# Silu in one activation for two token blocks, and weight chunks 29 to 40 assembled in SBUF instead of PSUM

## The chip, the cores and the metric

The kernel runs on one core of one Trainium2 chip. The core has five engines with an in-order queue each: TensorE (PE, matmuls, with its weight loads shown as PEld), VectorE (DVE), ScalarE (ACT), GpSimd (POOL) and SyncE (SP, which here only starts transfers). The metric is the time of one execution on the device in microseconds; lower is better.

## The reference

Three parts follow one another. All arithmetic of the reference is at float32 or better, and the weights come as float64.

```python
# attention: 2 x 8 heads, 768 tokens, head size 64; a query sees the keys of its hash bucket
scores = where(bucket(q) == bucket(k), q @ k.T / 8, -1e9)
x = softmax(scores) @ v                      # -> 1536 tokens x 512
# first feed-forward block, d_ff = 1536
xn = x / sqrt(mean(x * x) + 1e-6) * rms_g
g, val = xn @ w_gate, xn @ w_val
x = (g * (1 / (1 + exp(-g))) * val) @ w_out
# second feed-forward block, d_ff = 2048
r = maximum(x @ w_in, 0)
out = (r * r) @ w2_out
```

## The kernel before

**Precision.** Every float32 operand of a feed-forward matmul is split in a high part, which is rounded to the matmul's input format, and a low part, the rest. A product is then three matmuls: high x high, high x low, low x high. So weights and activations need two tiles each, and DVE makes the low parts by a subtraction (line 314).

**Token blocks.** The 1536 tokens are four blocks of 384 (`TB`). The first feed-forward block runs over blocks 0 and 1 while the second half of attention still runs (run 0), then over blocks 2 and 3 (run 1). The second feed-forward block then takes all four. Within a run the loop goes over 12 slices `f` of 128 hidden units. For a slice and a block PE makes the gate (`in_pe`, 12 matmuls of 384 columns, line 1012), then the value, also line 1012. Every two slices the output product follows (line 1108), whose result DVE adds to an accumulator in SBUF (line 1133).

**A gate and a value.** `gate_t` (line 1023) takes tanh(g/2) on ScalarE out of the PSUM bank into a tile `mt`. `gate_u` (line 1027) multiplies (mt + 1) with g, still in its bank, on DVE, into a tile `mu`. `val_u` (line 1032) multiplies with 0.5 and with the value. `y_hi` (a cast, ScalarE or GpSimd) and `y_lo` (a subtraction on DVE) split the result for the output product. There are three `mt` buffers and four `mu` buffers.

**Weights.** The weights are loaded as raw float64 chunks of 128 x 512 (512 KB each) and put together as float32 by integer operations: an absolute value of the upper words on ScalarE (`w_abs`, line 956), then four steps on DVE (`w_f32`: a clamp, line 962, a shift, line 967, and two that merge bits of the raw words, lines 972 and 976), a rounding cast (`w_hi`) and a subtraction (`w_lo`, line 314, DVE). There are 104 chunks, in the order of use: 36 of run 0 (gate, value, output for each slice), 36 of run 1 and 32 of the second block. There are three raw buffers (`wraw`). The tile on which the steps work is one of four in SBUF (`wv`), or, for chunks with an index in `WP = (6, 40)`, a PSUM bank (`mo`): `apart(m)` says which, and then the cast can only be ScalarE's, since GpSimd doesn't reach PSUM in this kernel. The banks `mo` are taken in turn, eight of them from the end of attention on, and the matmuls' results need them too.

**Order.** Nothing is ordered by the compiler. Each operation is given to a planner (`Plan`) with a rank, the engines that may do it, a cost on each (`D`, `A`, `P`, `T`), the buffers that it takes and frees, and whether it uses an SBUF port that DVE and GpSimd share (`port`). The planner plays a list schedule through by these costs and emits the instructions in that order; each engine then runs its own in order and waits by semaphores. A changed cost changes the order of everything that comes later.

Of the kernel before, what the change touches and what calls it, by code (L numbers as in the profile page):

```python
# [10 lines left out]
F32 = mybir.dt.float32  # L11
# [5 lines left out]
AF = mybir.ActivationFunctionType  # L17
ALU = mybir.AluOpType
# [3 lines left out]
B, H, S, D = 2, 8, 768, 64  # L22
# [7 lines left out]
TB = 384  # L30
# [24 lines left out]
WR = 3  # L55
WV = 4

WP = (6, 40)
MB = (3, 4)
G = 2  # L60

# [181 lines left out]
def tile_hash_attention_moe(  # L243
# [19 lines left out]
    nc = tc.nc  # L263
# [14 lines left out]
    where = {}  # L278
# [18 lines left out]
    add = plan.op  # L297
# [638 lines left out]
    def apart(m):  # L936

        return m in mats[WP[0]:WP[1]]

# [77 lines left out]
    def in_pe(eng, st, m, blk):  # L1017
        st["p"] = mo()[:, 0:TB]
        gemm_in(st["p"], m, xT[m[0], blk])

    def gate_t(eng, st):
        st["t"] = where["work"].tile([128, TB], F32, tag="mt", name="mt", bufs=MB[0])
        nc.scalar.activation(st["t"], st["p"], AF.Tanh, scale=0.5)

    def gate_u(eng, st, us):
        us["u"] = where["work"].tile([128, TB], F32, tag="mu", name="mu", bufs=MB[1])
        nc.vector.scalar_tensor_tensor(
            out=us["u"], in0=st["t"], scalar=1.0, in1=st["p"], op0=ALU.add, op1=ALU.mult
        )

    def val_u(eng, st, us):
        nc.vector.scalar_tensor_tensor(  # L1032
            out=us["u"], in0=us["u"], scalar=0.5, in1=st["p"], op0=ALU.mult, op1=ALU.mult
        )

    def relu(eng, st):
        st["t"] = where["work"].tile([128, TB], F32, tag="mt", name="mt", bufs=MB[0])
        nc.scalar.activation(st["t"], st["p"], AF.Relu)  # L1038

    def square(eng, st, us):  # L1040
        us["u"] = where["work"].tile([128, TB], F32, tag="mu", name="mu", bufs=MB[1])
        nc.vector.tensor_tensor(out=us["u"], in0=st["t"], in1=st["t"], op=ALU.mult)  # L1042
# [17 lines left out]
    us_of = {}  # L1060

    def plan_y(key, rank, ub, us, st=None, tb=None):
        p, ring, _ = y_place(key)
        yb = ("y",) + key
        add(
            lambda e: y_hi(e, key, us, st), rank, r=[p, ("u", key)], use=[ub] + ([tb] if tb else []),
            new=[(ring, yb)], w=[("yh", key)], A=0.413, P=(0.481, 0.3),
        )
        add(
            lambda e: y_lo(e, key, us), rank, r=[("yh", key)], use=[ub, yb], w=[("yl", key)],  # L1070
            D=(0.47, H_LO), port=True,
        )

    def plan_in(what, m, blk, n, rank):
        st, b = {}, ("in", m, blk)
        which, f = m[0], m[1]
        add(
            lambda e: in_pe(e, st, m, blk), rank, new=[("mo", b)], T=2.08,
            use=[("w", m), ("xT", which, blk)], r=[("wl", m)] + [("xT", which, blk, c) for c in range(4)],
        )  # L1080
        rank += R_AFT
        if what == "val":
            us, ub = us_of.pop(blk), ("mu", blk, f)
            add(lambda e: val_u(e, st, us), rank, use=[b, ub], w=[("u", (1, blk, f))], D=0.47)
            plan_y((1, blk, f), rank, ub, us)
            return
        tb = ("mt", m, blk)
        us = {}
        if what == "gate":
            us_of[blk] = us  # L1090
            add(lambda e: gate_t(e, st), rank, r=["work"], use=[b], new=[("mt", tb)], A=0.385)
            add(
                lambda e: gate_u(e, st, us), rank, use=[b, tb], new=[("mu", ("mu", blk, f))], D=0.47,
            )
        else:
            ub = ("mu 2", blk, f)
            add(lambda e: relu(e, st), rank, r=["work"], use=[b], new=[("mt", tb)], A=0.385)
            add(lambda e: square(e, st, us), rank, use=[tb], new=[("mu", ub)], D=0.47, port=True)
            plan_y((2, blk, f), rank, ub, us, st, tb)
# [127 lines left out]
    def plan_all():  # L1227
# [30 lines left out]
        for x in products():  # L1258
            rank = J0 + spent / RATIO
            if x[0] == "out":  # L1260
                _, which, run, blk, fs, d = x
                ms = [(which, f, 2 if which == 1 else 1, run) for f in fs]
            else:
                ms = [x[1]]
            for m in ms:
                if m not in done:
                    done.add(m)
                    plan_weights(m, rank + R_W)
            if x[0] == "out":
                plan_out(which, run, blk, fs, d, rank)  # L1270
                spent += (0.49 if which == 1 else 0.65) * len(fs)
            else:
                plan_in(x[0], x[1], x[2], x[3], rank)
                spent += 1.96
# [60 lines left out]
```

## Time and profile before

| | |
|---|---|
| median of 3 runs | 837.7 us (836.83 to 839.05) |
| the profiled execution | 836.23 us |
| its span, first to last instruction | 834.4 us |
| mean granted clock of TensorE over the span | 0.982 of full speed |
| busy: PE, DVE, ACT, POOL | 793.3, 705.2, 452.4, 223.8 us |

The busy times are sums over the whole span. Attention fills about the first 325 us, with the first feed-forward block's run 0 woven into it; run 1 and the second block follow. A row of the timeline gives the start, the duration, the engine, the line, the operation with output and input tiles, and in brackets how long the engine stood idle before it and what ended that. An instruction's duration overlaps a little with the next one's on the same engine, so the step from start to start says what one costs in a full queue.

### The profile page before, as it was taken

Reading aid. Unit: us, or ns where it says so; the run is one execution under the profiler, and the core shown is the slowest. Engines: PE = TensorE matmul, PEld = TensorE weight load, DVE = VectorE, ACT = ScalarE, POOL = GpSimd, SP = SyncE. Lnnn points to the kernel's source line nnn. Section 1 sums busy time; section 2 is a strip of 40 time slices with the busy share of each in tenths; the row PEclk is TensorE's granted clock in tenths of the full one; section 3 lists DMA queues with packets and bytes.
Section 4 is the critical chain, followed back from the end, with each engine's and each line's share of the span. In section 5 each row is a group of like instructions: output and inputs, shape, how many; then the busy total and the mean of one; then the engine's idle time right before and its main releaser. Section 6 shows DMA issues by size and latency. Waiting matters only on the chain.

```text
span 834.4 us, 14958 instructions
## 1 busy us (share of the span) xinstructions
PE 793.3 (95%) x5633; PEld 721.5 (86%) x5633; DVE 705.2 (85%) x1393; ACT 452.4 (54%) x922; POOL 223.8 (27%) x195
## 2 busy tenths in 40 slices
PE   8998887899998998989999999999999999999998
PEld 4787776788887898988889999999899898998996
DVE  6996889798788789989999999999687787877764
ACT  5788887767888677433455344446542242332320
POOL 7578955556567444000000000000000000000000
PEclk8999999999999899999999999999999999999999
DMA  7577784589979797223324334333231120211003
GB/s 224 156 136 145 148 192 127 120 178 177 238 153 187 156 212 171 77 76 101 127 101 148 105 126 129 126 125 95 83 101 45 58 76 30 97 51 51 26 1 151
DMA packets 127728, 100.69 MB, mean 121 GB/s; under 512 B 106548, under 2 KB 108596, under 8 KB 127656
## 3 DMA queue, kind: packets, MB, share of 16 engines
q1 hardware_dynamic: 124160, 90.92, 43.2%
q10 hardware_dynamic: 3496, 8.81, 4.0%
q8 instruction: 44, 0.72, 0.4%
q14 instruction: 28, 0.23, 0.1%
HBM read 67.12 MB, written 3.15 MB: 84 GB/s over the span
## 4 chain that ended last, share of the span: by engine, by line
PE 71%; DVE 20%; ACT 3%; DMA 3%; issue 2%; POOL 1%; ACTq 0%; SPq 0%; DVEq 0%; POOLq 0%
PE mo L1012 33%; PE mo L1119 16%; PE mo L1108 8%; PE S L549 5%; PE O L623 4%; PE S L428 3%; DVE Pa L560 2%; DMA Ta<-hla 2%; DVE mo L962 2%; DVE acc L1133 1%; DVE mo L967 1%; DVE mo L972 1%; DVE Px L560 1%; DVE Tx L314 1%; DVE mo L976 1%
## 5 line engine op out<-in xcount | busy, mean ns | idle before, releaser
L314 POOL TENSOR_TENSOR hla<-Pa,hla 128x768 f16<-128x768 f32 x66 | 110.0, 1669 | 75.1 <-ACT hla L305 67.8
L1133 DVE TENSOR_TENSOR acc<-acc,mo 128x512 f32<-128x512 f32 (+1 forms) x164 | 101.0, 617 | 25.0 <-PE mo L1119 22.9
L549 PE MATMUL S<-k,q 76*128 76x384 f32 (+1 forms) x384 | 92.2, 365 | 12.3 <-DVE Pa L560 7.1
L1038 ACT ACTIVATE mt<-mo 128x384 f32<-128x384 f32 x64 | 31.3, 489 | 100.8 <-PE mo L1012 97.5
L549 PEld LDWEIGHTS S<-k,q 76*128 76x128 f32 (+1 forms) x384 | 65.8, 194 | 18.8 <-DVE Pa L560 9.3
L1119 PE MATMUL mo<-woh,yl 128*128 128x512 f32 x192 | 75.3, 392 | 0.0
L1119 PE MATMUL mo<-wol,yh 128*128 128x512 f32 x192 | 75.2, 392 | 0.0
L1119 PE MATMUL mo<-woh,yh 128*128 128x512 f32 x192 | 74.7, 389 | 0.0
L560 DVE TENSOR_SCALAR_CACHE_REDUCE Pa<-S 128x768 f32<-128x768 f32 x66 | 62.7, 950 | 10.9 <-PE S L549 10.2
L309 POOL TENSOR_SCALAR yh<-mu 128x384 fp32r<-128x384 f32 x20 | 10.8, 541 | 221.6 <-PE mo L1119 88.0
L1042 DVE TENSOR_TENSOR mu<-mt 128x384 f32<-128x384 f32 x64 | 35.4, 553 | 36.0 <-ACT mt L1038 35.9
L1108 PE MATMUL mo<-yh,woh 128*128 128x384 f32 x192 | 64.8, 337 | 0.7 <-ACT woh L305 0.7
L314 DVE TENSOR_TENSOR yl<-mu,yh 128x384 fp32r<-128x384 f32 x112 | 61.8, 559 | 4.1 <-POOL yh L309 2.6
L578 ACT ACTIVATE Pa<-Pa,b 128x768 f32<-128x768 f32 x66 | 62.0, 943 | 5.2 <-DVE sum L631 1.3
L1108 PE MATMUL mo<-yh,wol 128*128 128x384 f32 x192 | 64.5, 336 | 0.1
L1108 PE MATMUL mo<-yl,woh 128*128 128x384 f32 x192 | 64.2, 335 | 0.0
L309 POOL TENSOR_SCALAR wih<-wv 128x512 fp32r<-128x512 f32 x12 | 7.5, 627 | 209.1 <-ACT mt L1038 109.7
L956 ACT ACTIVATE wv<-wraw 128x512 f32<-128x512 f32 x70 | 46.6, 671 | 26.3 <-DMA wraw<-in_w 24.9
L305 ACT CAST hla<-Pa 128x768 f16<-128x768 f32 x66 | 55.0, 835 | 5.8 <-DVE wv L972 1.5
L1012 PE MATMUL mo<-xTAh,wih 128*128 128x384 f32 x160 | 55.2, 345 | 2.3 <-DVE acc L1133 2.3
L1012 PE MATMUL mo<-xTBh,wih 128*128 128x384 f32 x160 | 55.2, 345 | 2.1 <-DVE mu L1032 2.1
L1012 PE MATMUL mo<-xTAh,wil 128*128 128x384 f32 x160 | 54.5, 340 | 0.3 <-DVE wil L314 0.3
(167 smaller groups left out, 2343.8 us busy)
## 6 DMA issues: line engine op xcount, KB each, us to landing
wraw<-in_w SPq DMA_DIRECT2D x104, 512.0 KB
rk<-in_k ACTq DMA_DIRECT2D x14, 384.0 KB
vr<-in_v SPq DMA_DIRECT2D x8, 384.0 KB
out<-acc SPq DMA_DIRECT2D x12, 256.0 KB
q<-q SPq DMA_DIRECT2D x15, 192.0 KB
rq<-in_q ACTq DMA_DIRECT2D x14, 192.0 KB
Ta<-hla SPq DMA_TRANSPOSE x66
rk<-in_k SPq DMA_DIRECT2D x2, 384.0 KB
```

The source lines that it names most:

```text
L305: nc.scalar.copy(out_, in_)
L314: engine[eng].tensor_tensor(out=out_, in0=in0, in1=in1, op=ALU.subtract)
L549: nc.tensor.matmul(sp[:, hf, 0:TB], d[a][0:kr, t * 128:(t + 1) * 128], d[b2][0:kr, hf * TB:(hf + 1) * TB], start=(n == 0), stop=(n == 1),)
L560: nc.vector.tensor_scalar(out=e["P"].rearrange("p (a b) -> p a b", a=2), in0=e["sp"][:, :, 0:TB], scalar1=-1e9 / SCALE, scalar2=None, op0= ...
L578: nc.scalar.activation(e["P"], e["P"], AF.Exp, bias=e["b"], scale=SCALE)
L623: nc.tensor.matmul(d["O"][:, t, 0:w], T[:, a, :], b2[:, c, :], start=(c == 0 and n == 0), stop=(c == QT - 1 and n == 2),)
L956: nc.scalar.activation(t, f32(wst[m]["hi"]), AF.Abs)
L1012: nc.tensor.matmul(ps, a[:, c * 128:(c + 1) * 128], b2[:, c, :], start=(c == 0 and n == 0), stop=(c == 3 and n == 2),)
L1042: nc.vector.tensor_tensor(out=us["u"], in0=st["t"], in1=st["t"], op=ALU.mult)
L1108: nc.tensor.matmul(po, a[:, dc * 128:(dc + 1) * 128], b2, start=(j == 0 and n == 0), stop=(j == len(fs) - 1 and n == 2),)
L1119: nc.tensor.matmul(po, a[:, tt * 128:(tt + 1) * 128], b2, start=(j == 0 and n == 0), stop=(j == len(fs) - 1 and n == 2),)
L1133: nc.vector.tensor_tensor(out=ac, in0=ac, in1=st["p"], op=ALU.add)
```

## The change

Two things change. In run 1 (blocks 2 and 3, `m[3]` is 1) the gate is one Silu activation on ScalarE, from the PSUM bank straight into `mu`; `gate_u` is left out and the value's product is a plain multiplication. Run 0 keeps tanh. And `WP` ends at 28 instead of 40: the 29th to 40th chunks (the last eight of run 0 and the first four of run 1) are put together in SBUF tiles `wv`, as the chunks after them are already.

```diff
-WP = (6, 40)
+WP = (6, 28)
...
+    def gate_s(eng, st, us):
+        us["u"] = where["work"].tile([128, TB], F32, tag="mu", name="mu", bufs=MB[1])
+        nc.scalar.activation(us["u"], st["p"], AF.Silu)
+
+    def val_s(eng, st, us):
+        nc.vector.tensor_tensor(out=us["u"], in0=us["u"], in1=st["p"], op=ALU.mult)
+
...
-            add(lambda e: val_u(e, st, us), rank, use=[b, ub], w=[("u", (1, blk, f))], D=0.47)
+            add(lambda e: (val_s if m[3] else val_u)(e, st, us), rank, use=[b, ub], w=[("u", (1, blk, f))], D=0.47)
...
-        if what == "gate":
+        if what == "gate" and m[3]:
+            us_of[blk] = us
+            add(
+                lambda e: gate_s(e, st, us), rank, r=["work"], use=[b], new=[("mu", ("mu", blk, f))],
+                A=0.385,
+            )
+        elif what == "gate":
```

## Rows read from the trace of the kernel before

**Rows 1.** The page, busy us (share of the span) and instructions by engine.
```profile
PE 793.3 (95%) x5633; PEld 721.5 (86%) x5633; DVE 705.2 (85%) x1393; ACT 452.4 (54%) x922; POOL 223.8 (27%) x195
```

**Rows 2.** Busy time by stretch: us, PE, PEld, DVE, ACT, POOL, clock, DMA.
```profile
354.00:363.00 9.00, 6.73 (x39) 6.41 (x37) 8.72 (x17) 2.78 (x6) 0.00 (x0) 1.00 0.14 37
363.00:386.00 23.00, 22.24 (x116) 21.63 (x117) 19.86 (x36) 7.26 (x14) 0.51 (x1) 0.93 0.33 104
386.00:403.00 17.00, 14.87 (x77) 14.55 (x76) 16.28 (x30) 5.83 (x11) 0.51 (x1) 0.90 0.32 118
403.00:432.00 29.00, 26.86 (x151) 25.58 (x150) 28.93 (x58) 13.84 (x27) 0.51 (x1) 1.00 0.26 87
432.00:450.00 18.00, 18.00 (x106) 18.00 (x105) 17.11 (x32) 9.67 (x20) 2.60 (x4) 1.00 0.49 157
450.00:575.00 125.00, 124.99 (x721) 124.67 (x721) 122.97 (x250) 53.53 (x100) 5.45 (x9) 1.00 0.36 118
```

**Rows 3.** The chain of waits from 384 to 434 us: start, us, what.
```profile
385.92 0.53 DVE mu L1032
...
430.95 0.69 DVE wil L314
```

**Rows 4.** Timeline of PE, the matmuls ahead of which PE stood idle.
```profile
363.03 0.45 PE L1012 MATMUL mo<-xTAh,wih 128*128 128x384 f32 x1 [2.30 <-DVE acc L1133]
...
376.50 0.41 PE L1108 MATMUL mo<-yh,woh 128*128 128x384 f32 x1 [0.68 <-ACT woh L305]
...
397.40 0.44 PE L1012 MATMUL mo<-xTBh,wih 128*128 128x384 f32 x1 [2.13 <-DVE mu L1032]
...
409.71 0.44 PE L1012 MATMUL mo<-xTDh,wil 128*128 128x384 f32 x1 [0.75 <-DVE wil L314]
...
430.20 0.44 PE L1012 MATMUL mo<-xTDh,wih 128*128 128x384 f32 x1 [0.30 <-ACT wih L305]
431.68 0.44 PE L1012 MATMUL mo<-xTDh,wil 128*128 128x384 f32 x1 [0.86 <-DVE wil L314]
```

**Rows 5.** Waits of PE from 432 us to the end: us in total, times, longest.
```profile
PE mo L1012 <- DVE wil L314: 0.9, 1, 0.9
```

**Rows 6.** Timeline of DVE: steps on chunks in PSUM (mo) and SBUF (wv).
```profile
356.51 0.69 DVE L962 TENSOR_SCALAR mo<-mo 128x512 f32<-128x512 f32 x1
...
418.83 0.69 DVE L962 TENSOR_SCALAR mo<-mo 128x512 f32<-128x512 f32 x1
419.43 0.54 DVE L314 TENSOR_TENSOR xTGl<-acc,xTGh 128x384 fp32r<-128x384 f32 x1
...
425.68 0.41 DVE L962 TENSOR_SCALAR wv<-wv 128x512 f32<-128x512 f32 x1
426.01 0.68 DVE L972 SCALAR_TENSOR_TENSOR mo<-wraw,mo 128x512 uint32<-128x512 uint32 x1
```

**Rows 7.** Timeline of DVE: the first gate product of run 1 and what follows.
```profile
408.05 0.54 DVE L1027 SCALAR_TENSOR_TENSOR mu<-mt,mo 128x384 f32<-128x384 f32 x1
408.51 0.54 DVE L1133 TENSOR_TENSOR acc<-acc,mo 128x384 f32<-128x384 f32 x1
```

**Rows 8.** ScalarE: the table load (groups by line); timeline, run 1's first tanh.
```profile
L1230 ACT ACT_TABLE_LOAD x1 | 1.3, 1283 | 0.7 <-PEq L1322 0.7
...
405.59 0.49 ACT L1023 ACTIVATE mt<-mo 128x384 f32<-128x384 f32 x1 [1.35 <-PE mo L1012]
```

**Rows 9.** Timeline, a step of GpSimd and a step of DVE beside it.
```profile
420.70 0.51 POOL L309 TENSOR_SCALAR yh<-mu 128x384 fp32r<-128x384 f32 x1 [28.45 <-PE mo L1108]
...
420.83 0.93 DVE L976 SCALAR_TENSOR_TENSOR wv<-wraw,wv 128x512 uint32<-128x512 uint32 x1
```

**Rows 10.** Waits of SyncE's queue, 340 to 440 us: total, times, longest.
```profile
SPq L943 <- DVE mo L976: 73.2, 15, 10.7
```

## The prediction

> **What bounds the kernel now.** I read the busy times first. TensorE (PE) is busy 95% of the span and VectorE (DVE) 85% [rows 1]; two engines that close together call for a reading by stage. The diff touches gates of token blocks 2 and 3 and weight chunks counted from the 29th, so I looked for those in time: the 29th chunk has its clamp at 356.51 us, the 40th at 418.83 us [rows 6], and the first gate of block 2 runs at 405.59 us [rows 8]. The table of stretches was therefore cut at 354, 363, 386, 403 and 432 us and then to 575 us, where the last such gate has ended [rows 2].
>
> What to see in it is the number of matmuls. From 450 to 575 us, 721 matmuls start in 125 us at full clock, one per 0.1734 us, with no gap: that is PE's own pace. From 354 to 432 us there are 39 + 116 + 77 + 151 = 383; at that pace they need 66.4 us, and they take 78. So **11.6 us of PE time is lost there**: 2.2, 2.9, 3.6 and 2.8 us by stretch. Part of it is clock: a mean of 0.93 over 23 us is a loss of 1.6 us, 0.90 over 17 us one of 1.7 us. The two stretches with a lower clock are those that begin with, or hold, a long idle of PE, 2.30 us before 363.03 and 2.13 us before 397.40; the last one, with idles of under 0.9 us, has a clock of 1.00 [rows 2, 4].
>
> Then the chain of waits. From 385.92 us to the weight subtraction that starts at 430.95 us its pieces are almost all DVE's, 42.8 of 45.7 us (the first and the last of 91 pieces stand in [rows 3]); DVE is busy 16.28 of 17 and 28.93 of 29 us there [rows 2]. PE waits for DVE's accumulation, its gate product and its weight parts, or for a cast behind them: six waits of 0.3 us and more, 7.0 us in all [rows 4]. After 432 us PE waits once, 0.9 us [rows 5]. So time can be won between 354 and 432 us and hardly anywhere later, and what is won there reaches the end, because PE runs full from then on.
>
> **The change part by part.** *Chunks back in SBUF.* Twelve chunks, the 29th to the 40th, leave the PSUM banks. Of a chunk's five DVE steps the first two (the clamp, line 962, and the shift, line 967) get cheaper. In PSUM one takes 0.69 us and the next instruction starts 0.60 us after its start; in SBUF it takes 0.41 us and the next starts 0.33 us after [rows 6]. That is 0.27 us each, and 24 x 0.27 = 6.5 us of DVE time in all. Their places on the timeline: 3 before PE's wait ends at 363.03, 8 from there to 386, 7 from 386 to 403, 6 to 432. The other three steps stay near 0.68 us, as do the absolute value and the cast on ScalarE. The loads move with it: SyncE holds 15 loads until DVE has read an old raw buffer, 73.2 us in all [rows 10], so a faster DVE brings them earlier.
>
> *Silu.* Each of 24 gates loses one DVE instruction (line 1027), 0.54 us long, 0.46 us from its start to the next [rows 7]: 11.0 us. Only the four between 403 and 432 us lie on the chain, 1.8 us; the other twenty lie under a PE that has no gap [rows 2, 5], and are costed at nothing. Were that cover gone, they would be worth 9.2 us. The new product is a plain two-input multiply instead of one with a factor; the accumulation, also a two-input operation with one input in PSUM, takes 0.54 us, as long as the gate's [rows 7]: nothing. The Silu itself takes Tanh's place on ScalarE, 0.49 us [rows 8]. I take it as equal, since it has the same tile and only another function.
>
> *New waits.* The gate now takes its `mu` buffer on ScalarE, where the DVE step took it: at the first gate 405.59 instead of 408.05, 2.5 us earlier [rows 7, 8]. Were no buffer free, casts and absolute values behind it on ScalarE would wait up to that long, and DVE's weight steps for them. With four buffers for two blocks in flight I take nothing, 2.5 us as the bound. Its PSUM bank, on the other hand, comes free after ScalarE's step instead of DVE's.
>
> *Table.* The trace has one table load, 1.28 us, at the start [rows 8]; none of its rows shows whether Silu needs another. One such load lies ahead of the first gate, where ScalarE is idle 1.35 us [rows 8]. I take nothing, 1.3 us as the bound. The Trainium skill ("ScalarE: Activation LUTs", "What ACT_TABLE_LOAD costs") adds a drain and gives 2.66 us for a switch; by that the sum below would be up to 1.3 us smaller.
>
> *The port.* An operation of GpSimd (POOL) at 420.70 us overlaps a DVE step on an SBUF chunk that takes 0.93 us instead of 0.68 [rows 9]: 0.25 us. POOL has three operations between 354 and 432 us [rows 2], and the planner may send it the twelve casts of chunks that it couldn't reach in PSUM. The bounds are nothing and 15 x 0.25 = 3.8 us. I take two collisions, 0.5 us, since ScalarE, 13.84 of 29 us busy [rows 2], can keep the casts. The Trainium skill ("SBUF — State Buffer", "Who interferes with whom") says that a DVE instruction with two SBUF inputs and a GpSimd one exclude each other for a whole instruction, a rule that speaks against this part of the change. This row's 0.25 us is less than POOL's 0.51 us; by the whole instruction the two collisions would cost 1.0 us.
>
> *The sum by stretch.* To 363 us: 3 x 0.27 = 0.8 of 2.2 us; the idle stays long, so its clock drop stays. 363 to 386: beside the clock (1.6) 1.3 us are lost; eight cheaper steps (2.2 us) close them: 1.3. 386 to 403: six of the seven lie ahead of the 2.13 us wait: 1.6; the remaining idle is short, so I count the drop as gone: 1.7. 403 to 432: 6 x 0.27 + 4 x 0.46 = 3.4 us against 2.8 lost: 2.8. Together 8.2, less 0.5 for the port: **7.7 us**. The profiled execution took 836.23 us (span 834.4 and 1.8 around it), so 828.5; the median of the runs shown, 837.7, is 1.5 us higher, so I predict **830.0 us**. The bounds: all 11.6 us back gives 826.1; 8.2 less the port's 3.8 leaves 4.4 us and gives 833.3. What could carry it to the upper gain is not in the sum: twelve chunks fewer take their turn among the eight banks that PE also needs.
>
> **The rivals.** *Weights come too late.* The chain could pass from DVE's steps to the loads, since only three raw buffers exist. For it: 73.2 us of SyncE waits [rows 10]. Against it: those end with DVE, not with the transfer. If the two long idles of PE and their clock stayed (2.2 + 1.6 + 3.6 us), 11.6 - 7.4 = 4.2 us at most, and with half of the rest 2.1 us, would be won: 835.6, no difference that counts.
>
> *The order turns against it.* The order of all instructions is written anew by the planner from its costs, from about 355 us on. Its place would be 432 to 575 us, where DVE has only 0.9 and 2.0 us to spare [rows 2] and a late weight part stops PE. Price: an idle of 2.13 us and its clock drop, 1.7, about 3.8 each. Two of them eat the gain; from the third it is slower: 3 x 3.8 - 7.7 = +3.7, 841.4 us. Against it: the new order has less DVE work everywhere.
>
> *A table load at every gate.* If Silu's table lacks what the neighbours on ScalarE use (absolute value, copy, square), each gate costs a load there and one back, 24 x 2 x 1.28 = 61.6 us between 405 and 556 us. ScalarE has room for it (busy 13.84 of 29 us and 53.53 of 125 [rows 2]), so only what delays a cast counts; from three pairs on PE's path (7.7 us) the gain is gone, and with eight of them (20.5 us) it is +12.8: 850.5 us. By the Trainium skill ("ScalarE: Activation LUTs", "Table sets: the hidden batching unit") cheap functions are in every set, so one switch would do; no row here shows it.
>
> **How the numbers follow.** Forecast (826.1 to 833.3): 0.68. Late weights in part, with 2.5 to 4.4 us won: 0.09. Late weights in full, or what is won given back, no difference that counts: 0.12. A worse order: 0.07. Table loads: 0.04. A measurement of this kernel tells 0.3%, 2.5 us, from no change. Faster: 0.68 + 0.09 = 0.77; same 0.12; slower 0.11. Range: 826.0 to 836.5 leaves out the slower cases, the worse half of the unchanged ones and little below.
>
> **What would show it.** Lines 962 and 967 on `mo` 22 times each instead of 34, and 82 on `wv`; line 1027 24 times; one more table load, near 405 us; PE's count between 354 and 424 us near 383; the 397 us idle and its clock drop gone. The prediction is wrong if PE's idles stay with DVE no longer busy (loads), if new idles stand after 432 us (order), or if table loads number about 49.

## The result and the profile after

The changed kernel takes 828.51 us (median of four runs, 826.86 to 829.05), the kernel before, in the same runs, 838.38 us (836.83 to 839.82). The ratio is 0.9884, with a 95% interval of 0.9863 to 0.9906: **9.9 us faster**, 7.9 to 11.5 us by the interval. 830.0 was predicted, 7.7 us faster. The profiled execution has a span of 824.7 us, 9.7 us less than before.

The page of the changed kernel, busy us by engine, to be held against [rows 1]:

```profile
PE 789.0 (96%) x5633; PEld 718.3 (87%) x5633; DVE 688.2 (83%) x1369; ACT 459.1 (56%) x931; POOL 220.0 (27%) x187
```

DVE has 24 instructions fewer and 17 us less to do, PE the same 5633 matmuls. The groups by line of the changed kernel show the parts of the edit (instruction, count, busy us, mean ns, idle before; what was line 1027 is now line 1034, what was 1032 is 1039):

```profile
L962 DVE TENSOR_SCALAR wv<-wv 128x512 f32<-128x512 f32 x82 | 36.9, 452 | 4.8 <-ACT wv L956 4.5
...
L967 DVE TENSOR_SCALAR wv<-wv 128x512 uint32<-128x512 uint32 x82 | 35.8, 440 | 0.9
...
L962 DVE TENSOR_SCALAR mo<-mo 128x512 f32<-128x512 f32 x22 | 15.3, 694 | 3.6 <-ACT mo L956 3.6
...
L1039 DVE SCALAR_TENSOR_TENSOR mu<-mu,mo 128x384 f32<-128x384 f32 x24 | 13.1, 548 | 2.2 <-PE mo L1012 2.2
L1030 DVE TENSOR_TENSOR mu<-mu,mo 128x384 f32<-128x384 f32 x24 | 13.1, 547 | 0.1
L1034 DVE SCALAR_TENSOR_TENSOR mu<-mt,mo 128x384 f32<-128x384 f32 x24 | 13.1, 547 | 2.4 <-ACT mt L1023 2.3
...
L1027 ACT ACTIVATE mu<-mo 128x384 f32<-128x384 f32 x24 | 11.7, 489 | 12.6 <-PE mo L1012 12.6
L1023 ACT ACTIVATE mt<-mo 128x384 f32<-128x384 f32 x24 | 11.7, 487 | 7.8 <-PE mo L1012 7.7
...
L1027 ACT ACT_TABLE_LOAD x1 | 1.3, 1283 | 0.0
```

Silu (line 1027) lasts as long as the tanh (line 1023), the plain product (line 1030) as long as the one with a factor (line 1039), and there is one table load for all 24 gates. Busy time by stretch of the changed kernel, columns as in [rows 2]; the first three cuts are the same:

```profile
354.00:363.00 9.00, 9.00 (x54) 9.00 (x53) 8.56 (x17) 3.74 (x8) 0.51 (x1) 1.00 0.23 63
363.00:386.00 23.00, 23.00 (x134) 22.94 (x133) 22.21 (x45) 9.26 (x17) 1.32 (x2) 1.00 0.40 121
386.00:403.00 17.00, 16.15 (x93) 15.64 (x92) 15.85 (x34) 8.98 (x15) 0.01 (x1) 1.00 0.41 137
403.00:423.00 20.00, 19.40 (x111) 18.82 (x110) 19.97 (x44) 10.92 (x20) 0.79 (x1) 1.00 0.35 110
423.00:441.00 18.00, 17.68 (x101) 17.04 (x100) 16.88 (x33) 10.80 (x22) 1.31 (x2) 1.00 0.45 149
441.00:566.00 125.00, 125.00 (x723) 125.00 (x722) 116.85 (x233) 56.43 (x106) 2.30 (x4) 1.00 0.37 118
```

From 354 to 403 us PE runs 281 matmuls, where it ran 232 [rows 2]: 49 more, 8.5 us at 0.1734 us each. Both stretches with a lower clock are gone, and so are both idles of over 2 us [rows 4]. What waits PE has left, on its timeline:

```profile
402.62 0.44 PE L1012 MATMUL mo<-xTDh,wil 128*128 128x384 f32 x1 [0.85 <-DVE wil L314]
...
417.24 0.44 PE L1012 MATMUL mo<-xTDh,wil 128*128 128x384 f32 x1 [0.60 <-DVE wil L314]
...
426.22 0.44 PE L1121 MATMUL mo<-yh,woh 128*128 128x384 f32 x1 [0.21 <-ACT woh L305]
```

and the chain of waits around them:

```profile
396.99 1.28 ACT L1027
398.29 0.38 ACT mu L1027
398.71 0.67 ACT wv L956
399.40 0.43 DVE wv L962
...
420.12 4.40 DMA wraw<-in_w
```

The chain names the table load and, later, a weight load of 4.40 us. The experiments ask whether either costs anything.

**A sharper measure.** The fastest and the slowest execution of one kernel lie 2 to 6 us apart, more than several experiments are worth. Most of that lies in other parts: before 300 us the clock falls to its lower level (1.2 of 2.4 GHz) for pieces of 3.41 us whose number varies (at the end). So beside the median I give the time from the start of the 3,111th matmul to that of the 4,347th, of 5,633, read from the start times in each trace. Ratios are to the kernel before on the same chip in the same hours, whose median was 838.1 to 839.9 us. The stretch begins ahead of the 29th chunk and ends just after run 1, in the first slices of the second block, at 346.92 and 574.75 us before. From the 4,347th matmul to the last it was 255.48 us in every kernel here: whatever is won stays won. The stretch is one trace per kernel and has a scatter of its own, of half a us at least, as the Silu-only kernel shows below.

| kernel | ratio to before (95% interval) | median us | stretch us | against before |
|---|---|---|---|---|
| before | | 838.38 | 227.83 | |
| changed | 0.9884 (0.9863 to 0.9906) | 828.51 | 218.19 | -9.6 |
| SBUF only | 0.9914 (0.9888 to 0.9940) | 830.45 | 221.60 | -6.2 |
| Silu only | 0.9983 (0.9966 to 0.9999) | 837.19 | 227.28 | -0.6 |
| changed, slow steps | 0.9983 (0.9966 to 1.0000) | 837.12 | 227.29 | -0.5 |
| changed, bank held | 0.9905 (0.9881 to 0.9929) | 830.40 | 220.67 | -7.2 |
| changed, old order | 0.9902 (0.9874 to 0.9929) | 830.43 | 219.51 | -8.3 |
| changed, no table load | 0.9891 (0.9865 to 0.9917) | 829.66 | 218.28 | -9.6 |

The same start times tell where a kernel gets ahead. The next table gives by how many us a kernel starts the 3,222nd, 3,302nd, 3,377th, 3,526th and 4,347th matmul earlier than the kernel before, both counted from the 3,111th; the heads are the times of these matmuls in the kernel before. At these five places all kernels of the table have done the same matmuls.

| kernel | ahead at 371 us | 386 | 403 | 432 | 575 |
|---|---|---|---|---|---|
| changed | 4.1 | 5.3 | 9.3 | 10.2 | 9.6 |
| SBUF only | 4.2 | 5.4 | 9.4 | 7.6 | 6.2 |
| Silu only | -0.6 | -0.6 | -0.6 | 0.2 | 0.6 |
| changed, slow steps | 3.8 | 2.1 | 6.0 | 0.2 | 0.5 |
| changed, bank held | 2.9 | 4.2 | 7.6 | 10.8 | 7.2 |
| changed, old order | 3.8 | 3.8 | 7.8 | 8.0 | 8.3 |

### The profile page after: what moved, and what is told of

Read it like the earlier page. It is cut to its first block, busy times and chain, and to the rows that moved or that the text cites. A ratio compares the mean times of both kernels' runs of the same rounds, so it can differ in the third digit from the quotient of the medians.

```text
span 824.7 us, 14921 instructions
## 1 busy us (share of the span) xinstructions
PE 789.0 (96%) x5633; PEld 718.3 (87%) x5633; DVE 688.2 (83%) x1369; ACT 459.1 (56%) x931; POOL 220.0 (27%) x187
## 4 chain that ended last, share of the span: by engine, by line
PE 69%; DVE 21%; DMA 3%; issue 3%; ACT 3%; POOL 1%; SPq 0%; ACTq 0%; DVEq 0%; POOLq 0%
PE mo L1012 31%; PE mo L1132 16%; PE mo L1121 8%; PE S L549 5%; PE O L623 4%; PE S L428 3%; DVE Pa L560 2%; DMA Ta<-hla 2%; DVE acc L1146 2%; DVE Px L560 1%; PE mo L878 1%; DVE q L437 1%; DVE mo L962 1%; PE mo L597 1%; DVE wv L976 1%
## 5 line engine op out<-in xcount | busy, mean ns | idle before, releaser
L309 POOL TENSOR_SCALAR yh<-mu 128x384 fp32r<-128x384 f32 x19 | 11.5, 603 | 277.5 <-PE mo L1132 147.7
L956 ACT ACTIVATE wv<-wraw 128x512 f32<-128x512 f32 x82 | 54.1, 671 | 21.6 <-DMA wraw<-in_w 20.9
L976 DVE SCALAR_TENSOR_TENSOR wv<-wraw,wv 128x512 uint32<-128x512 uint32 x82 | 57.1, 698 | 0.4
L305 ACT CAST wih<-wv 128x512 fp32r<-128x512 f32 x42 | 26.1, 622 | 55.9 <-DVE wv L976 55.7
L972 DVE SCALAR_TENSOR_TENSOR wv<-wraw,wv 128x512 uint32<-128x512 uint32 x82 | 56.3, 688 | 0.7
```

The lines of the kernel that those rows point to most:

```text
L305: nc.scalar.copy(out_, in_)
L956: nc.scalar.activation(t, f32(wst[m]["hi"]), AF.Abs)
L972: nc.vector.scalar_tensor_tensor(out=t, in0=hi, scalar=0xC0000000, in1=t, op0=ALU.bitwise_and, op1=ALU.bitwise_or)
L976: nc.vector.scalar_tensor_tensor(out=t, in0=lo, scalar=29, in1=t, op0=ALU.logical_shift_right, op1=ALU.bitwise_or)
```

## The experiments

Two theories of the gain. **S**: DVE's steps on the twelve chunks became cheaper, and DVE set the pace there. **B**: the chunks no longer take turns among the eight PSUM banks for which PE waited. Both fit the two long idles of [rows 4], since both end with a DVE step that frees a bank.

**One part at a time.** Chunks 29 to 40 in SBUF, the gate still a tanh (this edit is against the kernel before, all others against the changed kernel):

```diff
-WP = (6, 40)
+WP = (6, 28)
```

> Chunks 29 to 40 in SBUF, the gate stays tanh. Theory S (cheaper DVE steps): 24 steps x 0.27 us give 0.8, 1.3, 1.6 and 1.6 us by stretch, and one clock drop of 1.7 us goes: 7.0 us, less 0.5 for the port, 6.5 us under the kernel before, about 832. Theory B (PSUM banks): both long idles of PE (2.3 and 2.1 us) are waits for a bank, so both go with their clock drops whatever the steps cost: 7.8 us and more, 830 or below. If the Silu is what counts: within 2.5 us of before.

Measured: 0.9914, that is 7.2 us (5.0 to 9.4 by the interval), and 6.2 us in the stretch. That is near the 6.5 of theory S, but the way there isn't: neither long idle is left, as theory B had it, and the kernel is 9.4 us ahead by 403 us, where S had 5.4; after that it loses 3.2 us, where S had 1.6 more. So the total agrees with S by luck, and this run alone doesn't tell the theories apart. And the Silu, with the chunks in PSUM:

```diff
-WP = (6, 28)
+WP = (6, 40)
```

> Silu in blocks 2 and 3, chunks 29 to 40 stay in PSUM. Theory S: four gate products of 0.46 us lie on the chain, 1.8 us under before, about 836.5, and both long idles with their clock drops stay, since they lie ahead of the first Silu. Theory B: the same within 1 us; the gate's bank is free up to 2.5 us earlier, but only after 403 us. A Silu that is worth more than it lies on the chain: under 835.

Measured: 0.9983, 0.6 us in the stretch. The two longest waits of PE in this kernel from 340 to 435 us:

```profile
PE mo L1012 <- DVE acc L1146: 2.9, 1, 2.9
PE mo L1012 <- DVE mu L1039: 2.1, 1, 2.1
```

Both long idles stay, and at both the clock drops. Up to the first Silu this kernel runs the same instructions as the one before, and yet its first long idle is 2.9 us instead of 2.3, since a weight load landed later. The absolute value that waited for it, first before, then here:

```profile
353.58 0.63 ACT L956 ACTIVATE mo<-wraw 128x512 f32<-128x512 f32 x1 [1.09 <-DMA wraw<-in_w]
...
353.38 0.63 ACT L956 ACTIVATE mo<-wraw 128x512 f32<-128x512 f32 x1 [1.64 <-DMA wraw<-in_w]
```

So 0.6 us of its stretch is scatter, and without that the Silu alone would have given 1.1 us, still less than the 1.8 us it takes off DVE. On top of the moved chunks it gives 221.60 - 218.19 = 3.4 us. Half of those is a clock drop: the kernel with the chunks alone has one of 3.41 us at half speed, after this wait,

```profile
PE mo L1012 <- ACT wih L305: 1.8, 1, 1.8
```

and the changed kernel has none in this stretch. Of the other half, 0.8 us is a wait near the end of run 1 that the kernel with the chunks alone has and the changed kernel hasn't:

```profile
549.68 0.44 PE L1108 MATMUL mo<-yh,wol 128*128 128x384 f32 x1 [0.83 <-DVE wol L314]
```

**The steps at their old price.** The banks stay free, DVE works as long as before (`moved(m)` is true for chunks 29 to 40, and the planner gets the old price of these steps):

```diff
             nc.vector.tensor_scalar(
                 out=t, in0=t, scalar1=TINY, scalar2=HUGE, op0=ALU.max, op1=ALU.min
             )
+        if n < 2 and moved(m):
+            nc.vector.tensor_scalar(
+                out=t[:, 0:384], in0=t[:, 0:384], scalar1=TINY, scalar2=HUGE, op0=ALU.max,
+                op1=ALU.min,
+            )
...
```

> The changed kernel, with a second clamp over 384 of the 512 columns behind each of the two cheap steps of chunks 29 to 40, about 0.27 us each, so that DVE works as long as with the chunks in PSUM, but no bank is taken. Theory S: only the Silu's 1.8 us are left, 836 to 837, with PE's long idles back. Theory B: the idles stay away and at least 7 us of the 9.9 are kept, 829 to 831.

Measured: 0.9983, 0.5 us in the stretch. Nothing is left of the gain but what the Silu alone gives, so banks that are free don't give it by themselves. On DVE's timeline the added clamp costs 0.27 us from start to start, as meant:

```profile
360.30 0.36 DVE L970 TENSOR_SCALAR wv<-wv 128x384 f32<-128x384 f32 x1
360.57 0.55 DVE L1155 TENSOR_TENSOR acc<-acc,mo 128x384 f32<-128x384 f32 x1
```

Where PE's time goes, by stretch:

```profile
354.00:363.00 9.00, 9.00 (x54) 9.00 (x53) 7.34 (x16) 2.74 (x5) 0.00 (x0) 1.00 0.20 58
363.00:386.00 23.00, 21.12 (x115) 19.53 (x114) 22.62 (x49) 8.44 (x16) 0.62 (x1) 1.00 0.35 115
386.00:403.00 17.00, 17.00 (x100) 17.00 (x100) 16.73 (x39) 5.58 (x10) 1.43 (x2) 1.00 0.29 94
403.00:432.00 29.00, 24.48 (x117) 22.87 (x117) 27.77 (x57) 14.95 (x26) 1.73 (x2) 0.88 0.33 109
```

Neither long idle of [rows 4] is back, as theory B had it, and from 386 to 403 us PE doesn't stop: by 403 us it is 6.0 us ahead. But the time comes back in smaller waits, and from 403 to 432 us PE runs 117 matmuls where it ran 151 in the kernel before, with the clock at 0.88: 5.8 of the 6.0 us are gone. The waits there:

```profile
405.32 0.45 PE L1130 MATMUL mo<-yh,wol 128*128 128x384 f32 x1 [0.40 <-DVE wol L314]
...
406.61 0.44 PE L1130 MATMUL mo<-yh,woh 128*128 128x384 f32 x1 [0.85 <-ACT woh L305]
...
408.11 0.61 PE L1130 MATMUL mo<-yh,wol 128*128 128x384 f32 x1 [0.88 <-DVE wol L314]
...
427.44 0.44 PE L1021 MATMUL mo<-xTDh,wih 128*128 128x384 f32 x1 [1.72 <-ACT wih L305]
...
428.73 0.69 PE L1021 MATMUL mo<-xTDh,wil 128*128 128x384 f32 x1 [0.67 <-DVE wil L314]
```

Here the banks decided where PE stood idle, and DVE's work how long it did in all. This kernel's order was planned anew with the old prices; what that order does by itself was not told apart.

**The bank kept.** The steps stay cheap, but each of the twelve chunks takes a bank (the planner is told of it in lines not shown):

```diff
         nc.scalar.activation(t, f32(wst[m]["hi"]), AF.Abs)
+        if moved(m):
+            held[m] = mo()
+            nc.scalar.copy(held[m][:, 0:1], warm)
...
         copy(eng, wspl[m][0], wst[m]["v"])
+        if moved(m):
+            nc.scalar.copy(warm, held.pop(m)[:, 0:1])
```

> The changed kernel, but each of chunks 29 to 40 also takes a PSUM bank from its absolute value to its cast, held by a copy of one column on ScalarE at either end, and its cast stays on ScalarE. The steps keep their SBUF price. Theory S: the gain stays, 829 to 831. Theory B: PE waits for banks again, at 360 and 395 us with the clock drops: 5 us or more of the gain are lost, 834 to 837.

Measured: 0.9905; 7.2 of the 9.6 us in the stretch stay. Neither long idle is back, and by 432 us this kernel is 10.8 us ahead, as far as the changed one. What it loses comes after. PE's longest wait is for ScalarE, which here has 24 copies more and all casts of these chunks:

```profile
425.97 0.44 PE L1130 MATMUL mo<-yh,woh 128*128 128x384 f32 x1 [1.71 <-ACT yh L305]
```

and a drop of the clock of 3.41 us begins at 426.8 us. Those two, 1.7 us each, are more than the 2.5 us that this kernel loses to the changed one; how much of them is due to the banks and how much to the added copies was not told apart. The bank that is held is also not the full load of before: by the trace it is held for 7.6 us on average, from one copy to the other, where a chunk in the kernel before had its bank for 11.1 us, from the absolute value to the end of the subtraction. So with a bank held two thirds as long, a quarter of the gain at most goes; for the full time this isn't shown.

**The order.** The planner is told the old prices and buffers, so it writes the old order, and only what is emitted is new:

```diff
-        far = apart(m)
+        far = m in mats[6:40]
...
-            add(
-                lambda e: gate_s(e, st, us), rank, r=["work"], use=[b], new=[("mu", ("mu", blk, f))],
-                A=0.385,
-            )
+            add(lambda e: gate_s(e, st, us), rank, r=["work"], use=[b], new=[("mt", tb)], A=0.385)
+            add(lambda e: None, rank, use=[b, tb], new=[("mu", ("mu", blk, f))], D=0.47)
```

> The changed kernel with the order of before: the planner is told that chunks 29 to 40 still take PSUM banks at the old prices and that the gates still have two steps, so it writes the old order, and only what is emitted differs. If the gain is DVE work taken out of the stretch: 6 us or more under before, 829 to 832. If the new order is what gives it: under 3 us, 835 or above.

Measured: 0.9902; 8.3 us in the stretch. PE's matmuls come in the order of before, one by one. The new order is worth 1.3 us by the two traces, the lighter work and the free banks the rest.

**The table load.**

```diff
-        nc.scalar.activation(us["u"], st["p"], AF.Silu)
+        nc.scalar.activation(us["u"], st["p"], AF.Tanh)
```

> The changed kernel with Tanh in place of Silu as the one activation of the gate (the gate's function is then another), so that no second table load is needed; everything else is the same. The load is 1.28 us long and stands in the chain of waits at 397 us. If it sets the wait of 0.9 us that PE has at 401 us: 0.9 to 1.3 us under the changed kernel, 827 to 828. If DVE sets that wait anyway: equal to the changed kernel within 0.5 us.

Measured: 0.9891, and 218.28 us in the stretch where the changed kernel has 218.19. Without the load PE has the same wait before the same matmul, the 3,422nd; this execution is 2.5 us later here, nearly all of it from before the stretch:

```profile
405.08 0.45 PE L1012 MATMUL mo<-xTDh,wil 128*128 128x384 f32 x1 [0.84 <-DVE wil L314]
```

So the load costs nothing that the stretch can show, though the chain of waits named it: this wait is as long without it.

**What is late next.** Silu also from the eighth slice of blocks 0 and 1 on, after the last exp, and four raw buffers instead of three:

```diff
+FS = 7
...
-        if what == "gate" and m[3]:
+        if what == "gate" and (m[3] or f >= FS):
```

> The changed kernel with Silu also for blocks 0 and 1 from the eighth slice on, ten gates after the last exp, between 334 and 403 us: 10 x 0.46 = 4.6 us less DVE work there. If DVE's work is still what bounds that stretch: PE has lost only about 1 us from 354 to 423 us and 1.5 us just before, so 1 to 2.5 us under the changed kernel, 826 to 827.5. If the weight loads bound it now: equal within 1 us.

```diff
-WR = 3
+WR = 4
...
-    idle = const.tile([128, 512], F16, name="idle")
+    idle = xp.tile([128, 512], F16, name="idle")
```

> The changed kernel with four raw weight buffers instead of three (the warm-up matmuls' operand moves to another pool to make room). The chain of waits of the changed kernel has a load of 4.40 us at 420 us ahead of PE's last idles (0.9, 0.6 and 0.5 us from 416 to 427 us). If the loads are what is late next: 1 to 2 us under the changed kernel, 826.5 to 827.5. If DVE's steps are: equal within 1 us.

Measured: 0.9861 (0.9835 to 0.9887) and 0.9852 (0.9821 to 0.9884), intervals that overlap with the changed kernel's. (The waits that the second expectation names have 0.85, 0.60 and 0.21 us and end at 402.6, 417.2 and 426.2 us.) These edits also touch what comes ahead of the 3,111th matmul, and with four raw buffers the order of the matmuls differs from the 129th on. So here the stretch is taken from the 2,752nd, at 306.28 us before and the first behind 2,700 by which all these kernels have done the same matmuls, to the 4,347th: 268.47 us before, 258.80 changed, 256.87 with the early Silu, 260.00 with four raw buffers.

The early Silu is worth 1.9 us there, as expected if DVE's work still bounds that stretch. Four raw buffers fit neither expectation: the median, 825.08, lies below both, but in the stretch this kernel is 1.2 us slower than the changed one. The trace is of an execution of 829.28 us, while four of the six took 824.7 to 825.2 us. In it PE has two waits, at 343 and 350 us, the first with a clock drop behind it:

```profile
PE mo L1121 <- DVE wil L314: 2.4, 1, 2.4
PE mo L878 <- DVE wil L314: 1.4, 1, 1.4
```

Whether the faster executions have them isn't known, so what four raw buffers give stays open. Nor are late loads shown to be behind the changed kernel's last waits: those are gone with four raw buffers, but with the early Silu, too. Then the chunks: four more in SBUF,

```diff
-WP = (6, 28)
+WP = (6, 24)
```

> The changed kernel with four more chunks, the 25th to the 28th, in SBUF: 8 steps x 0.27 = 2.2 us less DVE work, between 318 and 357 us, where PE has waits of 1.8, 1.0 and 0.5 us. If the price of a step is what counts there too: 1 to 2 us under the changed kernel, 826.5 to 827.5. If that stretch is set by the end of attention: equal within 1 us.

and the combinations:

> The changed kernel with the 25th to 28th chunk in SBUF and Silu from the eighth slice of blocks 0 and 1 on. If the two add: 2 to 4 us under the changed kernel, 824.5 to 826.5. If PE's pace is reached after 354 us: no better than Silu from the eighth slice alone, about 826.5.

> The changed kernel with Silu from the eighth slice of blocks 0 and 1 on and four raw buffers. Alone they gave 1.4 and 1.7% under the kernel before, where the change itself gave 1.2%. If DVE work and late loads are two causes: 3 to 5 us under the changed kernel, 823.5 to 825.5. If both close the same waits: 825 to 826.5.

> All three: the 25th to 28th chunk in SBUF, Silu from the eighth slice of blocks 0 and 1 on, four raw buffers. If they add: 5 to 6 us under the changed kernel, 822.5 to 823.5. If PE's pace bounds it from 354 us on: as the kernel with the first two of them or the last two, whichever is lower.

| kernel | ratio to before (95% interval) | median us | from the 2,752nd matmul, us |
|---|---|---|---|
| `WP` to 24 | 0.9824 (0.9796 to 0.9853) | 825.01 | 254.65 |
| `WP` to 24, early Silu | 0.9807 (0.9780 to 0.9834) | 823.07 | 252.60 |
| early Silu, four raw buffers | 0.9860 (0.9833 to 0.9886) | 826.95 | 258.13 |
| all three | 0.9781 (0.9753 to 0.9809) | 820.46 | 254.60 |

Four more chunks in SBUF are worth 4.2 us in the stretch, twice what was expected, and the early Silu 2.0 more, so that the two together also give more than the 2 to 4 us expected; whether the four chunks win by the price of their steps or by their banks was not tested. The third row reaches neither of its expectations. The last row is the fastest kernel here, 2.2% under the kernel before and lower than expected. In the stretch, though, four raw buffers make it 2.0 us slower than the second row, and the third row 1.3 us slower than the early Silu alone. So what they give, if anything, lies ahead of the stretch, where the order is another one; the intervals of the second and the last row overlap, and no run tells the two apart. PE's waits from 300 to 420 us with `WP` to 24 and the early Silu, where the kernel before had 7.0 us from 354 to 432 us alone:

```profile
PE O L624 <- DVE sum L632: 0.4, 1, 0.4
```

## Why the prediction was right, point by point

**What bounds it: right.** The gain lies between 354 and 432 us and reaches the end. The bound of 11.6 us held, though it was read a little low: the 383 matmuls of [rows 2] count those that lie across a cut in both stretches; 377 start there, and by these 12.5 us were lost. From 354 to 424 us the changed kernel's count is 392, where near 383 was named as a sign: it is further ahead than forecast.

**Chunks in SBUF: right in mechanism.** The price per step, 0.27 us times 24, was needed for the gain: put back, it took the gain away, with the banks still free. But the freed banks set where the time is won, and the sum had nothing for them: the chunks alone are 9.4 us ahead by 403 us and keep 6.2.

**Silu: the place right, the size not.** Predicted 1.8 us; about 1.1 us alone, and 3.4 us on top of the moved chunks, of which 1.7 is the drop that no longer comes. The other twenty gates were costed at nothing because PE has no gap above them. With the chunks moved that cover has a hole: without Silu PE waits 0.8 us at 549 us, with it not. Beside the kernel before they give nothing, as predicted: PE's full stretch, 125 us, has as many matmuls as before.

**The sum by stretch: two terms were mis-sized, in opposite directions.** By the table above the changed kernel is ahead by 4.1 us after PE's first long idle and its clock drop (predicted 0.8), by 1.2 more at 386 us (1.3), by 4.0 more at 403 us (3.3) and by 0.3 more at the end of run 1 (2.8, less 0.5 for the port). The first term was 3.3 us too small, the last 2.0 too large; that the total was out by only 2 us is in part luck. The first term failed in "the idle stays long, so its clock drop stays". That idle was not a backlog to be worked off 0.27 us at a time: it is gone in the kernel whose steps are slow but whose banks are free, and gone in the one with cheap steps and the old order. The last term took all the lost time of 403 to 432 us as won. But in the changed kernel PE still waits there, 0.85, 0.60 and 0.21 us, for weight parts and a cast behind DVE, which is busy 19.97 of 20 us from 403 to 423 us. The chain names a load of 4.40 us ahead of the last of these waits; that late loads are the cause isn't shown, since the early Silu removes these waits as well. The rival of late weights, by which the two long idles stay, did not come.

**Table: right.** One load of 1.28 us, at 396.99 us, worth nothing that the stretch can show. From the load's start to Silu's it is 1.30 us; the extra drain of the Trainium skill ("ScalarE: Activation LUTs", "What ACT_TABLE_LOAD costs") does not show. One load serves 24 gates with casts, absolute values and copies between them. That agrees with the Trainium skill ("ScalarE: Activation LUTs", "Table sets: the hidden batching unit"), which has copy and the absolute value in every set.

**Port: right.** GpSimd has four operations from 354 to 423 us on its timeline, at 360.34, 384.13, 385.30 and 406.14 us, and two of them meet a step on a chunk in SBUF:

```profile
360.54 0.85 DVE L976 SCALAR_TENSOR_TENSOR wv<-wraw,wv 128x512 uint32<-128x512 uint32 x1
...
384.33 0.71 DVE L962 TENSOR_SCALAR wv<-wv 128x512 f32<-128x512 f32 x1
```

The first takes 0.17 us over the usual 0.68, the second 0.30 over the usual 0.41: two collisions and 0.5 us, as the prediction took. One cast of these chunks went to GpSimd, where the bound had twelve.

**The worse order:** it didn't come; by the two traces the new order is 1.3 us better than the old one.

## What to carry to other kernels

When two engines are near full, find the stretch in which each one is, count the other's instructions there against its own best pace, and price an edit only where the loaded engine's work lies on the chain. A buffer that stands in the way may only move the idle time: give the loaded engine its work back at the old price, and see whether the gain stays. Price where a scratch tile lies, PSUM or SBUF, stretch by stretch: here twelve chunks moved back were worth 6.2 us by themselves, and four more 4.2 us. And add up a forecast by stretch, then check it by stretch: two errors of 2 and 3 us hid in a total that was out by 2.

## What the runs showed of the hardware that was not expected

TensorE's granted clock falls to half, 1.2 GHz, in pieces of 3.41 us, or two or three of them in a row, each a loss of 1.7 us where PE is busy. Between 345 and 575 us such a piece came after a single wait of PE of 1.7 to 2.9 us (2.30 and 2.13 before, 1.72, 1.71 and 1.8 in three experiments) or, once, after three waits of 0.40, 0.85 and 0.88 us that ended at 405.3, 406.6 and 408.1 us; a lone wait of 0.9 us had none behind it. Size alone doesn't decide: a wait of 1.92 us at 328 us of the kernel before had none either, and neither had the longest of all, 2.91 us, in the kernel with the early Silu and four raw buffers, where the granted clock stays at 1.00:

```profile
350.11 1.60 PE L879 MATMUL mo<-diag,xall 128*128 128x128 f32 x12 [2.91 <-DVE wil L315]
```

And the same instructions up to 300 us had a different number of such pieces in different executions: 23.9 us at the lower clock in four of the profiles of the first table, 27.3 in two, 30.7 in two. That moves the 2,700th matmul between 298.7 and 302.6 us, and it is why a stretch between two counted matmuls told the experiments apart better than their medians did.

Such a stretch has two limits that showed here. A weight load that landed later moved it by 0.6 us with the same instructions. And it compares the same work only where the kernels have done the same matmuls by its first one: by the 2,700th the kernels with four raw buffers had done 22 other matmuls than the rest, and measured from there the four buffers would have seemed to gain 0.5 us where they lose 1.2.
